# An order of work for a fused attention, soft MoE and routed MoE kernel: state loads on SyncE, the first step, pass changes and the first routed slots re-ordered

## The chip, the cores and the metric

The kernel runs on one core of one Trainium2 chip. The time is that of one launch on the device, in microseconds (us), from the runs' own clock; the profile's span is the time from the first to the last instruction of one profiled execution. The engines are TensorE (PE in the profile, its weight loads PEld), VectorE (DVE), ScalarE (ACT), GpSimd (POOL) and SyncE (SP), which only issues transfers here. Every engine works through its own instructions strictly in order.

## The reference

Three stages follow each other. N = 4 x (512 + 32) = 2176 tokens of 512 numbers, D = 64 per head, 8 heads, E = 8 experts with a hidden layer of F = 1024, all in float32.

```python
# stage 1: per batch and head, x (512 x 64) reads a state (32 x 64) and the state reads x
a  = softmax(x @ state.T / sqrt(64));  xread = a @ state
a2 = softmax(state @ x.T / sqrt(64));  sread = a2 @ x
x = concat([xread, sread], axis=2).transpose(0, 2, 1, 3).reshape(N, 512)
# stage 2: soft MoE, gates balanced by 8 Sinkhorn rounds
P = exp(x @ w_gate - max)
for _ in range(8):
    P /= P.sum(1); P /= P.sum(0); P *= N / E
x = sum(P[:, e:e+1] * (relu(x @ w1[e]) @ w2[e]) for e in range(E))
# stage 3: each token goes to its best expert alone
e = argmax(x @ w_gate2);  g = softmax(x @ w_gate2)[e] * sigmoid(x @ w_output_gate)[e]
out = g * (relu(x @ w1_2[e]) @ w2_2[e])
```

## The kernel before

**Tiling.** The 2176 tokens are 17 tiles of 128. Stage 2 goes over them in three passes, `PASSES` (first token, half width): (0, 384), (768, 384), (1536, 320), so passes have 6, 6 and 5 tiles. A pass has 32 steps: 8 experts by 4 quarters of 256 of the hidden layer. To keep float32 accuracy with the fast matmul type, every operand is split in a high part (a cast, on ScalarE) and a low part (operand minus high part, on VectorE or GpSimd), and each product is three matmuls (high by high, high by low, low by high; L481 to L483).

**A step** `s` has two halves. `mm1(s)` forms the hidden layer as seven products of a Strassen-like scheme, 6 matmuls each, from sums of quarters of the weights and of the tokens; between the products ScalarE copies and applies relu (L499, L490) and VectorE adds and forms low parts (L507 to L531, L494). In all steps but the first, the product numbered 2 comes fifth; in step 0 it comes second. `mm2(s)` multiplies the hidden layer by the second weights, tile by tile, 6 matmuls into one bank (L563 to L565), and VectorE adds the bank, weighted by the gate, into `acc` (L581; raw in the first experts, L572). The loop does `mm1` of step s and then `mm2` of step s - 1, so that TensorE has work while the hidden layer is finished.

**Operands one step ahead.** SyncE loads a quarter of the first weights (L418) and of the second (L421) into `rawb`. `prep_w1(s)` forms the sums on GpSimd (L434 to L437), the high parts on ScalarE (L438, L439, L442) and the low parts on GpSimd (L444, L446, L448); it runs inside step s - 1. `prep_w2(s)` casts on ScalarE (L458) and subtracts on GpSimd (L459); it runs inside `mm1(s)`, after its second product. Token operands of a pass are made by `xsums` and `xsplit`: seven operands, each cast on ScalarE (L406) and its low part formed on VectorE or GpSimd (L408); `pool` in `xsplit` names the operands whose low part is GpSimd's.

**Filling in.** `queue` is a list of closures; `pump` is called after every product and tile with the TensorE time that went by, and takes an item from the list whenever that credit reaches `pace`. The list holds the attention of batches 2 and 3 (`window(b)`, 17 items each: c0 to c4 of the two halves of the heads, and parts of the earlier batch), the 17 gate products, then the Sinkhorn rounds (`balance`), later the routing tables. In step 0 five items are taken directly in `between`. `todo` and the dictionary given to `step_mm2` do the same for the last two steps of a pass: the next pass's token operands (`xsplit`), and per finished tile `final_a` (store to x1d and x1p, L591 and L596, transposes L599, copy L601) and `final_b` (routing logits L610, L611).

**The order is written by hand** (`manual_schedule`): instructions are issued per engine in the order of the code, and what waits, waits for data or for a buffer. The first two batches' attention, with idle matmuls of no effect between, stands ahead of step 0. State of a batch comes by `load_state`: a memset on VectorE (L142), then four loads per half of the batch list, which ScalarE issues (L145). Batches 2 and 3 are loaded just ahead of step 0.

**Stage 3.** Tokens are routed to slots of 128 rows of one expert. VectorE builds tables (route parts `Rq[c][0..2]` for chunks c of tiles, L642 to L704; block tables in `blocks`, L1149 to L1187), TensorE turns them into row lists (`btab`: L715, then `indices`, L719 to L722), and GpSimd gathers a slot's rows (L834). `xT` transposes them (L842), with high part on ScalarE (L844) and low part on VectorE (L845); `m1` is the first layer (L855 to L857), `hT` transposes its relu (L869, L872, L873), `m2s` is the second layer (L880 to L882), scaled by the gate (L886) and scattered (L887). `load_w`/`split_w` bring the next expert's weights (L756, L806, L807). The gates of the slots come by a second table (`gmul` on GpSimd, L1198; `gtab` on TensorE, L715 into `pgat`). The head of this stage, slots 0 and 1, reads:

```python
m1(0, (seq(A[16], Rq[3][0]), seq(Bq[15], Bq[16]), seq(Rq[4][0], Rq[3][1])))
xT(1)
m1(1, (seq(Rq[4][1], blocks, lambda: load_w(2, 0)), lambda: hT(0)))
m2s(0, (None, btab, lambda: gather(2), seq(Rq[3][2], Rq[4][2], gmul)))
hT(1)
```

where the functions in brackets are called after the first, second, ... group of products of the layer.

Of the kernel before, what the change touches and what calls it, by code (L numbers as in the profile page):

```python
# [21 lines left out]
def tile_state_attention_moe_moe2(  # L22
# [117 lines left out]
    def load_state(b):  # L140
        stp = ap2.tile([P, G, P], F32, tag="stp", name=f"stp{b}")
        nc.vector.memset(stp, 0.0)  # L142
        sv = state[b].rearrange("(g q) s d -> q s g d", q=4)
        for q in range(4):
            nc.scalar.dma_start(out=stp[NS * q : NS * (q + 1), :, D * (q % 2) : D * (q % 2) + D], in_=sv[q])  # L145
        stps[b] = stp
# [250 lines left out]
    def xsplit(p, t, order=(0, 4, 3, 5, 1, 2, 6)):  # L397
        pool = (3, 1, 6) if p > 0 else ()
# [439 lines left out]
    def xT(sl):  # L838
# [5 lines left out]
        nc.scalar.copy(M["xh"], pv)  # L844
        nc.vector.tensor_tensor(out=M["xl"], in0=pv, in1=M["xh"].bitcast(F32), op=ALU.subtract)  # L845

    def m1(sl, hooks=()):
        ps2 = [bank(f"pm{sl}_{n}") for n in range(2)]
        hi, lo = M["xh"], M["xl"]
# [57 lines left out]
    with tc.manual_schedule():  # L907
# [9 lines left out]
        load_raw(0, 0)  # L917
        load_x(1, 0, accf[:, 2048:3072])
        load_state(1)
        gate_constants()  # L920
        load_raw(0, 1)
# [5 lines left out]
        load_x(1, 1)  # L927
        A1[0]()
# [21 lines left out]
        C0[3]()  # L950
        sums, T0 = xsums(0, accf)
        parts = xsplit(0, T0, (0, 1, 4, 3, 5, 2, 6))
        parts[0]()
        C1[3]()
        C0[4]()
        C1[4]()
        parts[1]()
        sums[0]()
        sums[1]()
        parts[2]()  # L960

        early = {0: [parts[3], sums[2]], 4: [parts[4]], 1: [parts[5], sums[3]], 2: [parts[6]]}
# [41 lines left out]
        def close_reads():  # L1004
# [6 lines left out]
            pace[0] = 5.6  # L1011
# [11 lines left out]
        def first_rows():  # L1023
# [3 lines left out]
            M["xh"], M["xl"] = (XR[:, 16384 + 512 * i : 16896 + 512 * i].rearrange("p (k t) -> p k t", k=KD) for i in (0, 1))  # L1027
# [8 lines left out]
        def step_mm1(s):  # L1036
            h = PASSES[s // NU][1]
            nxt = prep_w1(s + 1) if s < LAST else [lambda: None] * 2

            def between(i):  # L1040
                if s == 0:
                    for f in early.get(i, ()):
                        f()
                    if i in (0, 4, 1, 2, 3):
                        queue.pop(0)()
                if i == 1:
# [33 lines left out]
        queue += [gate([t]) for t in (6, 7, 0, 1, 2)] + spread(window(2), [3, 4, 5], 4)  # L1080
# [6 lines left out]
        pace[0] = 132.0 / (len(queue) - 5)  # L1087
# [3 lines left out]
        for s in range(3 * NU):  # L1091
# [29 lines left out]
            if p < 2:  # L1121
# [6 lines left out]
                step_mm2(s, {ts[2]: [a[0]], ts[3]: [a[1]], ts[4]: [b[0], a[2]], ts[5]: [b[1], a[3]]})  # L1128
# [4 lines left out]
            else:  # L1133
# [4 lines left out]
                step_mm2(s, {13: [A[12]], 14: [A[13], Bq[12]], 15: [A[14], Bq[13]],  # L1138
                             16: [piece[6], Bq[14], A[15], piece[7], lambda: xT(0)]})
# [70 lines left out]
        xT(1)  # L1210
        m1(1, (seq(Rq[4][1], blocks, lambda: load_w(2, 0)), lambda: hT(0)))
        m2s(0, (None, btab, lambda: gather(2), seq(Rq[3][2], Rq[4][2], gmul)))
# [61 lines left out]
```

## Time and profile before

| what | value |
|---|---|
| runs (3), us | 1844.94, 1847.14, 1849.73 |
| median | 1847.14 |
| the profiled execution: its own time / its span | 1845.63 / 1843.4 |
| TensorE busy, share of the span | 1787.8 us, 97% |
| VectorE / ScalarE / GpSimd busy | 1219.0 (66%) / 653.2 (35%) / 1086.4 us (59%) |
| mean granted clock of TensorE | 0.982 |

The span is the profiled execution from its first to its last instruction; its own time is 2.2 us longer, for what lies around the program. Busy time of TensorE counts an instruction at either clock as busy, so a stretch at half the clock looks full: the granted clock (1.00 is 2.4 GHz, 0.50 is 1.2 GHz) has to be read beside it. In timeline rows the bracket at the end gives the idle time of the engine just before the instruction and what ended it.

### The profile page before, as it was taken

How to read it: one execution, taken by the hardware profiler on the slowest of the kernel's cores; microseconds unless marked ns; L12 is line 12 of the kernel's file. 1: busy time of each engine (PE TensorE's matmuls, PEld its weight loads, DVE VectorE, ACT ScalarE, POOL GpSimd, SP SyncE). 2: the span in 40 equal slices, each digit the busy share in tenths (PEclk: the TensorE clock that was granted, in tenths of full speed). 3: DMA queues.
4: the chain of work that ended last, by engine and by line, in shares of the span. 5: the costliest groups of instructions: out<-in, count | busy, mean ns of one | idle time of the engine just before them, and what ended most of it. 6: DMA issues, size and time to landing. Idle time of an engine off the chain costs nothing.

```text
span 1843.4 us, 25573 instructions
## 1 busy us (share of the span) xinstructions
PE 1787.8 (97%) x9365; PEld 1594.5 (86%) x9365; DVE 1219.0 (66%) x2064; ACT 653.2 (35%) x1114; POOL 1086.4 (59%) x851
## 2 busy tenths in 40 slices
PE   7899998999999999999999999999999999899998
PEld 5889887899999889999999998889999998678886
DVE  5667679976676686666666666897666666545332
ACT  3334332233333433333333333333333334245333
POOL 1445445576776666666667765677787877222212
PEclk8799999999999999999999999999999999899999
DMA  4323421123222322112222222232222222335122
GB/s 108 82 92 81 114 65 55 60 69 101 60 71 68 121 74 68 66 66 65 69 98 69 69 69 92 81 126 81 81 81 81 81 80 81 115 106 195 44 83 91
DMA packets 126619, 154.67 MB, mean 84 GB/s; under 512 B 41424, under 2 KB 91600, under 8 KB 123920
## 3 DMA queue, kind: packets, MB, share of 16 engines
q1 hardware_dynamic: 121920, 142.41, 24.4%
q0 software_dynamic: 3280, 10.23, 1.6%
q8 instruction: 77, 1.26, 0.3%
q14 instruction: 62, 0.51, 0.1%
q10 hardware_dynamic: 1280, 0.26, 0.1%
HBM read 138.99 MB, written 14.42 MB: 83 GB/s over the span
## 4 chain that ended last, share of the span: by engine, by line
PE 71%; issue 12%; DVE 8%; DMA 4%; POOL 3%; ACT 1%; SPq 0%; POOLq 0%; DVEq 0%; ACTq 0%
PE py L563 12%; PE py L564 12%; PE py L565 12%; PE p L481 10%; PE p L483 10%; PE p L482 10%; DMA out_dram<-xst,si 2%; DVE HB L494 1%; DMA out_dram<-y,si 1%; DVE acc L581 1%; POOL XR L448 1%; PE psr L288 1%; PE pss L213 1%; POOL wl L459 1%; PE psg L310 1%
## 5 line engine op out<-in xcount | busy, mean ns | idle before, releaser
L459 POOL TENSOR_TENSOR wl<-rawb,wh 128x1024 fp32r<-128x1024 f32 x96 | 232.0, 2416 | 435.9 <-ACT wh L458 435.8
L481 PE MATMUL p<-XR 128*128 128x384 f32 (+1 forms) x1344 | 448.3, 334 | 9.0 <-ACT u L499 8.7
L483 PE MATMUL p<-XR 128*128 128x384 f32 (+1 forms) x1344 | 444.1, 330 | 9.2 <-POOL XR L448 8.1
L482 PE MATMUL p<-XR 128*128 128x384 f32 (+1 forms) x1344 | 442.7, 329 | 0.0
L563 PE MATMUL py<-wh,HB 128*128 128x512 f32 x1088 | 427.8, 393 | 2.2 <-DVE u L507 2.2
L565 PE MATMUL py<-wh,HB 128*128 128x512 f32 x1088 | 425.2, 391 | 0.0
L564 PE MATMUL py<-wl,HB 128*128 128x512 f32 x1088 | 425.1, 391 | 0.0
L581 DVE SCALAR_TENSOR_TENSOR acc<-py,PG,acc 128x512 f32<-128x512 f32 x461 | 321.2, 740 | 63.3 <-PE py L565 62.6
L448 POOL TENSOR_TENSOR XR<-sst,XR 128x1024 fp32r<-128x1024 f32 x96 | 252.4, 2629 | 56.4 <-ACT XR L442 56.4
L481 PEld LDWEIGHTS p<-XR 128*128 128x128 f32 x1344 | 256.1, 191 | 16.1 <-ACT u L499 8.8
L483 PEld LDWEIGHTS p<-XR 128*128 128x128 f32 x1344 | 255.6, 190 | 11.7 <-POOL XR L448 10.1
L494 DVE SCALAR_TENSOR_TENSOR HB<-u,HB 128x384 fp32r<-128x384 f32 (+1 forms) x192 | 186.7, 974 | 111.5 <-ACT HB L490 111.2
L482 PEld LDWEIGHTS p<-XR 128*128 128x128 f32 x1344 | 256.1, 191 | 3.3
L563 PEld LDWEIGHTS py<-wh,HB 128*128 128x128 f32 x1088 | 204.4, 188 | 44.5 <-DVE u L507 3.0
L565 PEld LDWEIGHTS py<-wh,HB 128*128 128x128 f32 x1088 | 204.2, 188 | 43.4
L564 PEld LDWEIGHTS py<-wl,HB 128*128 128x128 f32 x1088 | 204.4, 188 | 39.0
L499 ACT COPY u<-p 128x384 f32<-128x384 f32 (+1 forms) x96 | 44.3, 461 | 490.3 <-PE p L483 485.1
L444 POOL TENSOR_TENSOR XR<-rawb,XR 128x512 fp32r<-128x512 f32 x96 | 138.9, 1447 | 7.7 <-ACT XR L438 7.7
L442 ACT CAST XR<-sst 128x1024 fp32r<-128x1024 f32 x96 | 100.6, 1048 | 82.6 <-POOL sst L437 82.6
L490 ACT ACTIVATE HB<-u 128x384 fp32r<-128x384 f32 (+1 forms) x192 | 96.9, 505 | 77.9 <-DVE u L526 68.8
L507 DVE TENSOR_TENSOR u<-p,u 128x384 f32<-128x384 f32 (+1 forms) x96 | 51.2, 533 | 97.3 <-PE p L483 96.0
L490 ACT ACTIVATE HB<-p 128x384 fp32r<-128x384 f32 (+1 forms) x96 | 45.5, 474 | 181.6 <-PE p L483 181.6
(296 smaller groups left out, 2491.7 us busy)
## 6 DMA issues: line engine op xcount, KB each, us to landing
rawb<-in_moe_w_dram SPq DMA_DIRECT2D x192, 512.0 KB, 3.5
raw<-in_moe_w_dram SPq DMA_DIRECT2D x15, 1024.0 KB, 6.8
xb<-in_x_dram SPq DMA_DIRECT2D x60, 128.0 KB, 3.4
rawb<-in_moe_w_dram SPq DMA_DIRECT2D x5, 1024.0 KB, 5.0
x1d<-acc SPq DMA_DIRECT2D x16, 256.0 KB, 2.7
xtd<-xtm SPq DMA_DIRECT2D x4, 512.0 KB, 2.8
x1p<-acc SPq DMA_DIRECT2D x8, 256.0 KB, 3.1
xst<-xtd SPq DMA_DIRECT2D x1, 1536.0 KB, 9.5
```

What stands on the lines that cost most here:

```text
L444: nc.gpsimd.tensor_tensor(out=wop(s, 1, 0, 2).rearrange(r, k=KD), in0=raw[:, :, 0:P], in1=wop(s, 0, 0, 2).rearrange(r, k=KD).bitcast(F32), ...
L448: nc.gpsimd.tensor_tensor(out=wop(s, 1, 3, 4), in0=sst.rearrange("p a c -> p (a c)"), in1=wop(s, 0, 3, 4).bitcast(F32), op=ALU.subtract)
L459: nc.gpsimd.tensor_tensor(out=lo, in0=raw, in1=hi.bitcast(F32), op=ALU.subtract)
L481: nc.tensor.matmul(ps, wh, xh, start=start and k == 0, stop=False, skip_group_check=True)
L482: nc.tensor.matmul(ps, wh, xl, start=False, stop=False, skip_group_check=True)
L483: nc.tensor.matmul(ps, wl, xh, start=False, stop=stop and k == 1, skip_group_check=True)
L490: nc.scalar.activation(out=hh[:, f, half * h : (half + 1) * h], in_=c, func=AF.Relu)
L494: nc.vector.scalar_tensor_tensor(out=hl[:, f, q], in0=c, scalar=0.0, in1=hh[:, f, q].bitcast(F32), op0=ALU.max, op1=ALU.subtract)
L563: nc.tensor.matmul(ps, hh[:, j, r], whi[:, j, :], start=(j == 0), stop=False)
L564: nc.tensor.matmul(ps, hh[:, j, r], wlo[:, j, :], start=False, stop=False)
L565: nc.tensor.matmul(ps, hl[:, j, r], whi[:, j, :], start=False, stop=(j == 1))
L581: nc.vector.scalar_tensor_tensor(out=a, in0=ps, scalar=PG[:, t, e : e + 1], in1=a, op0=ALU.mult, op1=ALU.add)
```

## The change

It changes the order of work and which engine does some of it; what is computed stays the same.

- States of batches 2 and 3 are loaded from SyncE instead of ScalarE.
- In the prologue the first weights' loads and the gate constants come later, the second batch's loads earlier. Of the token operands of pass 0, the second is split ahead of the last attention parts; two of seven low parts go to GpSimd; the operands and sums are spread anew over step 0's products (`early`).
- The queue starts with gates 0 to 7, all of which are taken in step 0 (8 items instead of 5), and then the whole window of batch 2 without gates in it. The pace is 132/(length - 8), where it was 132/(length - 5): 132/56 and 132/59. Behind the attention it is 5.2 instead of 5.6.
- At pass changes (steps 32 and 64), `prep_w2` of the pass's first step and `prep_w1` of its second are called after tiles of the last `mm2` of the pass before, and no longer in the `mm1` of the first step.
- There are two buffers for a slot's transposed rows (`M["x"]`). `xT(0)` stands behind tile 14 and `xT(1)` behind tile 16 of the last `mm2`; before, `xT(0)` stood behind tile 16 and `xT(1)` behind `m1(0)`. In `m1(1)`, `hT(0)` comes ahead of `blocks`, and in `m2s(0)` the row table comes after the seventh group of products, the gather of slot 2, the rest of the routing and `gmul` after the eighth; they were behind the second, third and fourth.

```diff
@@ load_state
-            nc.scalar.dma_start(out=stp[...], in_=sv[q])
+            (nc.scalar if b < 2 else nc.sync).dma_start(out=stp[...], in_=sv[q])
@@ xsplit
-        pool = (3, 1, 6) if p > 0 else ()
+        pool = (3, 1, 6) if p > 0 else (3, 2)
@@ xT, m1
-        nc.scalar.copy(M["xh"], pv)
-        nc.vector.tensor_tensor(out=M["xl"], in0=pv, in1=M["xh"].bitcast(F32), op=ALU.subtract)
+        xh, xl = M["x"][sl == 1]
+        nc.scalar.copy(xh, pv)
+        nc.vector.tensor_tensor(out=xl, in0=pv, in1=xh.bitcast(F32), op=ALU.subtract)
...
-        hi, lo = M["xh"], M["xl"]
+        hi, lo = M["x"][sl == 1]
@@ prologue
         load_x(0, 1)
-        load_raw(0, 0)
         load_x(1, 0, accf[:, 2048:3072])
         load_state(1)
-        gate_constants()
-        load_raw(0, 1)
+        load_raw(0, 0)
...
         load_x(1, 1)
+        gate_constants()
+        load_raw(0, 1)
...
         C1[2]()
-        C0[3]()
         sums, T0 = xsums(0, accf)
         parts = xsplit(0, T0, (0, 1, 4, 3, 5, 2, 6))
         parts[0]()
+        C0[3]()
+        parts[1]()
         C1[3]()
         C0[4]()
+        sums[0]()
         C1[4]()
-        parts[1]()
-        sums[0]()
         sums[1]()
-        parts[2]()
-        early = {0: [parts[3], sums[2]], 4: [parts[4]], 1: [parts[5], sums[3]], 2: [parts[6]]}
+        early = {0: [parts[2], parts[3]], 4: [sums[2]], 1: [parts[4], sums[3]], 2: [parts[5], parts[6]]}
@@ close_reads
-            pace[0] = 5.6
+            pace[0] = 5.2
@@ first_rows
-            M["xh"], M["xl"] = (XR[:, 16384 + 512 * i : ...] for i in (0, 1))
+            M["x"] = [[h[:, o + 512 * i : ...] for i in (0, 1)] for h, o in ((XR, 16384), (HB, 2048))]
@@ step_mm1
-            nxt = prep_w1(s + 1) if s < LAST else [lambda: None] * 2
+            ahead = s > 0 and s % NU == 0
+            nxt = prep_w1(s + 1) if s < LAST and not ahead else [lambda: None] * 2
...
-                    if i in (0, 4, 1, 2, 3):
+                    for _ in range((1, 1, 1, 1, 3, 1, 0)[i]):
                         queue.pop(0)()
-                if i == 1:
+                if i == 1 and not ahead:
                     prep_w2(s)
@@ the queue
-        queue += [gate([t]) for t in (6, 7, 0, 1, 2)] + spread(window(2), [3, 4, 5], 4)
+        queue += [gate([t]) for t in (0, 1, 2, 3, 4, 5, 6, 7)] + window(2)
...
-        pace[0] = 132.0 / (len(queue) - 5)
+        pace[0] = 132.0 / (len(queue) - 8)
@@ the last step of a pass
-                step_mm2(s, {ts[2]: [a[0]], ts[3]: [a[1]], ts[4]: [b[0], a[2]], ts[5]: [b[1], a[3]]})
+                w1a, w1b = prep_w1(s + 2)
+                step_mm2(s, {ts[0]: [lambda: prep_w2(s + 1)], ts[1]: [w1a], ts[2]: [a[0]], ts[3]: [a[1], w1b],
+                             ts[4]: [b[0], a[2]], ts[5]: [b[1], a[3]]})
...
-                step_mm2(s, {13: [A[12]], 14: [A[13], Bq[12]], 15: [A[14], Bq[13]],
-                             16: [piece[6], Bq[14], A[15], piece[7], lambda: xT(0)]})
+                step_mm2(s, {13: [A[12]], 14: [A[13], Bq[12], lambda: xT(0)], 15: [A[14], Bq[13], piece[6]],
+                             16: [lambda: xT(1), Bq[14], A[15], piece[7]]})
@@ slots 0 and 1
-        xT(1)
-        m1(1, (seq(Rq[4][1], blocks, lambda: load_w(2, 0)), lambda: hT(0)))
-        m2s(0, (None, btab, lambda: gather(2), seq(Rq[3][2], Rq[4][2], gmul)))
+        m1(1, (Rq[4][1], lambda: hT(0), seq(blocks, lambda: load_w(2, 0))))
+        m2s(0, (None,) * 6 + (btab, seq(lambda: gather(2), Rq[3][2], Rq[4][2], gmul)))
```

Line numbers of the changed kernel lie one higher from `xT` on (L842 is L842, L845 is L846, L873 is L874), and some more at the end.

**First step, ScalarE.** The rows run from the end of the last attention part (copies into `xst`, L254) to the second weights' cast (`wh`, L458). Before:

```order
L254 COPY xst<-pso_402 128x256
L254 COPY xst<-pso_406 128x256
L406 CAST XR<-xst 128x768
L406 CAST XR<-acc 128x768
L145 DMA stp_427<-in_state_dram 32x2x64 x4
L145 DMA stp_433<-in_state_dram 32x2x64 x4
L499 COPY u_103<-p_0_446 128x384
L406 CAST XR<-acc 128x768
L490 ACTIVATE HB<-p_0_446 128x384
L406 CAST XR<-acc 128x768
L406 CAST XR<-xst 128x768
L458 CAST wh_496<-rawb 128x1024
```

and in the changed kernel:

```order
L254 COPY xst<-pso_405 128x256
L254 COPY xst<-pso_409 128x256
L499 COPY u_103<-p_0_444 128x384
L406 CAST XR<-acc 128x768 x2
L490 ACTIVATE HB<-p_0_444 128x384
L406 CAST XR<-acc 128x768
L458 CAST wh_506<-rawb 128x1024
L406 CAST XR<-xst 128x768
```

The eight state loads (two rows of four) are gone from the place ahead of the copy of `u`, one token operand is cast ahead of the attention's end, and between the copy of `u` and the weights' cast there are three token operands in both orders.

**First pass change, GpSimd.** The rows run from the last low part of the sums (L448) of the old pass's prepared step to the end of the preparation for the new pass's second step (`raw` and `xst` hold the new pass's tokens and sums). Before:

```order
L448 TENSOR_TENSOR XR<-sst,XR 128x1024
L408 TENSOR_TENSOR XR<-raw_2243,XR 128x768
L408 TENSOR_TENSOR XR<-xst,XR 128x768
L408 TENSOR_TENSOR XR<-raw_2243,XR 128x768
L459 TENSOR_TENSOR wl_5380<-rawb,wh_5379 128x1024
L434 TENSOR_TENSOR sst<-rawb 128x256
L435 TENSOR_TENSOR sst<-sst,rawb 128x256
L436 TENSOR_TENSOR sst<-rawb 128x256
L437 TENSOR_TENSOR sst<-rawb,sst 128x256
L444 TENSOR_TENSOR XR<-rawb,XR 128x512
L446 TENSOR_TENSOR XR<-rawb,XR 128x256
L448 TENSOR_TENSOR XR<-sst,XR 128x1024
```

and in the changed kernel:

```order
L448 TENSOR_TENSOR XR<-sst,XR 128x1024
L408 TENSOR_TENSOR XR<-raw_2243,XR 128x768
L459 TENSOR_TENSOR wl_5240<-rawb,wh_5239 128x1024
L434 TENSOR_TENSOR sst<-rawb 128x256
L435 TENSOR_TENSOR sst<-sst,rawb 128x256
L436 TENSOR_TENSOR sst<-rawb 128x256
L437 TENSOR_TENSOR sst<-rawb,sst 128x256
L408 TENSOR_TENSOR XR<-xst,XR 128x768
L444 TENSOR_TENSOR XR<-rawb,XR 128x512
L446 TENSOR_TENSOR XR<-rawb,XR 128x256
L448 TENSOR_TENSOR XR<-sst,XR 128x1024
L408 TENSOR_TENSOR XR<-raw_2243,XR 128x768
```

The weights' low part and the sums stand behind one token operand instead of three, the other two lie among and behind the weights' low parts.

**Tail, VectorE.** The rows show where the low half of the first slot's hidden layer (HB, L873 before, L874 in the change) stands relative to the block tables. Before, behind all of them (here their last four):

```order
L1184 TENSOR_SCALAR sm_13845<-sm_13844,sm_9838 128x24
L1185 TENSOR_SCALAR sm_13847<-sm_13845 128x24
L1186 TENSOR_TENSOR esel<-sm_13845,sm_13847 128x24
L1187 TENSOR_SCALAR flag<-sm_13829 128x1
L873 TENSOR_TENSOR HB<-pt_0_13888,HB 128x512
L821 UNCONDITIONAL_BRANCH
L873 TENSOR_TENSOR HB<-pt_1_13895,HB 128x512
```

and in the changed kernel ahead of them (L1154 is the first of the block tables there):

```order
L687 TENSOR_SCALAR rt_rb<-rt_rki 128x2
L688 CAST bk<-rt_rb 128x2
L874 TENSOR_TENSOR HB<-pt_0_13819,HB 128x512
L874 TENSOR_TENSOR HB<-pt_1_13826,HB 128x512
L1154 TENSOR_TENSOR sm_13843<-prank_13790,k_70 128x136
L1156 TENSOR_REDUCE sm_13839<-sm_13843 128x8
L1157 TENSOR_TENSOR sm_13839<-sm_13839,sm_10255 128x8
L1158 TENSOR_TENSOR sm_13844<-lowr,sm_13839 128x64
```

## Rows read from the trace of the kernel before

**Rows 1.** The page's 40 equal slices of the span: granted TensorE clock in tenths.

```profile
PEclk8799999999999999999999999999999999899999
```

**Rows 2.** Stretches: us, busy of PE, PEld, DVE, ACT, POOL; clock, DMA share, GB/s.

```profile
50.00:70.00 20.00, 19.34 (x72) 19.34 (x73) 11.91 (x20) 7.74 (x12) 9.46 (x8) 0.51 0.20 56
150.00:200.00 50.00, 50.00 (x293) 44.01 (x292) 36.46 (x64) 16.17 (x32) 20.00 (x16) 1.00 0.31 83
320.00:325.00 5.00, 3.78 (x12) 3.78 (x13) 4.83 (x11) 0.00 (x0) 4.61 (x6) 0.50 0.30 105
640.00:650.00 10.00, 7.86 (x35) 7.11 (x34) 7.69 (x14) 5.08 (x11) 7.10 (x5) 0.83 0.25 85
1150.00:1160.00 10.00, 6.79 (x34) 6.53 (x35) 7.08 (x14) 3.99 (x10) 7.70 (x6) 0.83 0.16 53
1580.00:1590.00 10.00, 8.66 (x44) 7.00 (x45) 4.48 (x20) 1.78 (x7) 0.00 (x0) 0.83 0.05 11
1600.00:1620.00 20.00, 16.33 (x79) 14.02 (x78) 12.37 (x49) 6.10 (x6) 5.81 (x6) 0.83 0.56 204
```

**Rows 3.** Timeline of the first step: start us, us, engine, instruction, [idle before <- releaser].

```profile
46.38 3.71 ACTq L145 DMA_DIRECT2D stp<-in_state_dram  x8
...
50.13 0.48 ACT L499 COPY u<-p 128x384 f32<-128x384 f32 x1 [5.05 <-DMA stp<-in_state_dram]
...
50.66 0.69 PE L481 MATMUL p<-XR 128*128 128x384 f32 x1 [8.73 <-ACT u L499]
...
54.23 0.96 DVE L408 TENSOR_TENSOR XR<-acc,XR 128x768 fp32r<-128x768 f32 x1 [0.95 <-ACT XR L406]
...
55.95 2.35 POOL L459 TENSOR_TENSOR wl<-rawb,wh 128x1024 fp32r<-128x1024 f32 x1 [21.61 <-ACT wh L458]
...
57.09 2.03 DVE L408 TENSOR_TENSOR XR<-xst,XR 128x768 fp32r<-128x768 f32 x1
...
69.62 2.37 POOL L448 TENSOR_TENSOR XR<-sst,XR 128x1024 fp32r<-128x1024 f32 x1 [4.51 <-ACT XR L442]
...
72.05 0.45 PE L483 MATMUL p<-XR 128*128 128x384 f32 x1 [1.15 <-POOL XR L448]
...
84.70 0.95 PE L310 MATMUL psg<-wg,xst 128*128 128x8 f32 x8
```

**Rows 4.** Timeline of the two pass changes.

```profile
628.88 1.82 POOL L408 TENSOR_TENSOR XR<-raw,XR 128x768 fp32r<-128x768 f32 x1 [7.76 <-DMA x1d<-acc]
...
635.38 2.38 POOL L459 TENSOR_TENSOR wl<-rawb,wh 128x1024 fp32r<-128x1024 f32 x1 [4.67 <-ACT wh L458]
...
645.61 0.45 PE L483 MATMUL p<-XR 128*128 128x384 f32 x1 [2.14 <-POOL XR L448]
...
1150.87 0.42 PE L483 MATMUL p<-XR 128*128 128x320 f32 x1 [1.16 <-POOL XR L444]
...
1154.36 0.41 PE L483 MATMUL p<-XR 128*128 128x320 f32 x1 [2.34 <-POOL XR L448]
```

**Rows 5.** Waits of TensorE, 250 to 360: us in total, times, longest us.

```profile
PE pscol L344 <- DVE sm L339: 9.6, 4, 5.2
```

**Rows 6.** Timeline of the first two slots of stage 3.

```profile
1580.69 0.50 PE L855 MATMUL pm<-XR 128*128 128x512 f32 x1 [1.68 <-ACT XR L844]
...
1582.07 0.79 PE L857 MATMUL pm<-XR 128*128 128x512 f32 x1 [0.64 <-DVE XR L845]
...
1593.01 0.50 PE L855 MATMUL pm<-XR 128*128 128x512 f32 x1 [1.32 <-ACT XR L844]
...
1604.22 0.50 PE L882 MATMUL pY<-XR,HB 128*128 128x512 f32 x1 [3.67 <-DVE HB L873]
...
1608.69 0.18 DVE L719 TENSOR_SCALAR gi<-ptab 128x24 int32<-128x24 f32 x1 [3.92 <-PE ptab L715]
...
1613.35 1.71 POOL L1198 TENSOR_TENSOR osg<-sm,gsplit 128x408 fp32r<-128x408 bf16 x2 [3.21 <-DVE gsplit L703]
...
1615.29 2.06 PE L715 MATMUL pgat<-osg,ohj 128*128 128x48 f32 x17
```

**Rows 7.** Waits of TensorE, 0 to 100.

```profile
PE psa L238 <- DVE e L233: 3.6, 3, 1.3
```

More of the change, by code (lines that the diff above doesn't have):

```diff
@@ L144, in load_state @@
         for q in range(4):
-            nc.scalar.dma_start(out=stp[NS * q : NS * (q + 1), :, D * (q % 2) : D * (q % 2) + D], in_=sv[q])
+            (nc.scalar if b < 2 else nc.sync).dma_start(out=stp[NS * q : NS * (q + 1), :, D * (q % 2) : D * (q % 2) + D], in_=sv[q])
         stps[b] = stp
@@ L1026, in first_rows @@
             M["y"] = [xst[:, 2560:3072], None]
-            M["xh"], M["xl"] = (XR[:, 16384 + 512 * i : 16896 + 512 * i].rearrange("p (k t) -> p k t", k=KD) for i in (0, 1))
+            M["x"] = [[h[:, o + 512 * i : o + 512 * i + 512].rearrange("p (k t) -> p k t", k=KD) for i in (0, 1)]
+                      for h, o in ((XR, 16384), (HB, 2048))]
             M["hh"], M["hl"] = (HB[:, 1024 * i : 1024 * i + 1024].rearrange("p (j t) -> p j t", j=NJ) for i in (0, 1))
```

## The prediction

> **What bounds it now.** I read four views in this order. The page's slices show TensorE's granted clock at 9 nearly everywhere and at 7 or 8 only at the front and in the tail [rows 1]; TensorE itself is busy 97% of the span. So the time is TensorE's work, plus the places where it stops or runs at the low clock. A table of stretches then finds those places [rows 2]: the steady stretch 150 to 200 is 50.00 busy of 50.00 at clock 1.00, and there nothing can be won. The first step (50 to 70) is busy too, but at 0.51, that is at 1.2 instead of 2.4 GHz; it gives up 20 x 0.49 = 9.8 us. The pass changes (640, 1150) and two places of the tail (1580, 1600) show 0.83, and 320 to 325 shows 0.50 with only 3.78 of 5.00 busy. The timeline then names what each place waits for [rows 3, 4, 6], and the chain of waits gives the sums [rows 5, 7].
>
> In the first step the story starts on ScalarE [rows 3]: eight state loads sit in its queue from 46.38, for 3.71 us, because they wait for a memset behind VectorE's work. The copy of u, next in that queue, starts at 50.13 after 5.05 idle, and TensorE stands 8.73 us before 50.66, its product long done. Then it works on at the low clock. GpSimd's chain (second weights, sums, low parts) is late in turn, and step 1's second product gets its operand only at 72.05.
>
> At the pass changes [rows 4] GpSimd is idle 7.76 and 4.67 us before the end of a pass and then late: TensorE stops 2.14, and 1.16 + 2.34 at the second change. In the tail [rows 6] TensorE stops 1.68 and 0.64 at the first slot's rows, 1.32 at the second's, and 3.67 for the hidden layer's low half, which stands on VectorE behind the block tables.
>
> **The change, part by part.** The sum is made against the profiled execution, 1845.63 us (span 1843.4). The median of the runs, 1847.14, lies 1.5 above it.
>
> *Front (state loads, first step, gates).* With the loads on SyncE, the u copy follows its product: that ended at 50.66 - 8.73 = 41.93, so u starts near 42.1, 8.0 earlier than 50.13. From u to the second weights' low part on GpSimd the trace has 5.8 us (50.13 to 55.95); the new order has the same three operands in between, and part of the 5.8 waits for half-clock products, so I take 5.6: it starts at 47.7, 8.25 earlier. From there to the end of the low part that step 1 waits for, the trace has 69.62 + 2.37 - 55.95 = 16.0 us. In it are 4.51 of waiting for ScalarE's cast, which waits on TensorE's half-clock products; that goes. One more operand's low part comes onto GpSimd in this stretch, 1.82 us by its row at the pass change [rows 4]; the other moved one runs ahead of the weights, in idle time. So 16.0 - 4.5 + 1.8 = 13.3, end at 61.0 instead of 72.0: 10.9 won. GpSimd then bounds this step and TensorE stops in pieces, so three more gates (8 instead of 5) fall in idle time: 3 x 0.95 = 2.85 at most, nothing at least; I take 2.4, since an 11 us shorter step still has stops of some 5 us by this working. Those stops may hold the clock low for a while beyond what the chain hides: 0 to half of the 9.8, and I take 1.5, because the products behind GpSimd's chain are hidden by it. Front: 10.9 + 2.4 - 1.5 = 11.8, ends 5 (rival A below, with one gate's 0.8 less hidden) and 13.8 (all gates, no clock loss).
>
> What stands behind the moved loads on SyncE is the next w2 quarter (L421), which needs a buffer that the weights' low part frees later anyway: nothing. The prologue's other moves (weights' first load behind the x and state loads) are covered by the idle matmuls there; GpSimd was idle 21.61 before its low part at 55.95, so a load some us later costs nothing.
>
> What a DMA on ScalarE costs is shown by the row: the issue takes 3.71 us, but the copy behind it is held 5.05 and TensorE 8.73 [rows 3]. The Trainium skill, "DMA: Bandwidth & Descriptors", section "Issuing engines are not separate DMA queues", says that issuing from several engines saves only the sequencer's time, usually small. By it the move would be worth 3.71, the front 3.7 + 2.4 - 1.5 = 4.6, and the time about 1826. I keep the row: it shows a queue that waits, not only issues.
>
> *Sinkhorn (265 to 325).* Before, TensorE waits 9.6 us in 4 for VectorE's chain [rows 5], the longest 5.2, and 320 to 325 has clock 0.50 [rows 2]. The change moves gates out of the attention windows and sets the pace behind it at 5.2 instead of 5.6, so the column sums come at other points of the steps. VectorE is 4.83 of 5.00 busy there, so the chain itself gets no shorter. The bounds: all of the longest wait and most of the clock go (7), or one more wait of 2 comes. I take 2.5, about the half-clock loss of that one stretch (5 x 0.50).
>
> *Pass changes.* GpSimd's work for the new pass's first two steps (low part 2.38, sums, low parts) moves ahead into its 7.76 + 4.67 of idle time. What can go: at the first change 2.14 and 10 x 0.17 = 1.7 of clock, at the second 1.16 + 2.34 + 1.7: together 9.0. Less 1 for VectorE and ScalarE, whose copies and accumulations for the last tiles now stand behind four more casts: 8. Ends 4 (half of the waits only move) and 9.
>
> *Tail.* Gone: 1.68 + 0.64 + 1.32 + 3.67 = 7.3 of stops [rows 6], as both slots' rows are ready before the pass ends and the hidden layer stands before the block tables; and the low clock, 10 x 0.17 + 20 x 0.17 = 5.1 [rows 2]. New: the gate products now start late. From the indices at 1608.69 to the end of the gate products 1613.35 + 1.71 = 1615.06 there are 6.37 us that ran beside the first slot's second layer; now only its last three matmuls and one transpose block lie beside them (about 1.7), so TensorE stops some 4.7 before the gate table at 1615.29, and the clock costs about 2 after it. 12.4 - 4.7 - 2 = 5.7, ends 2 (the stop 8, nothing hidden) and 9 (fully hidden second table, one clock loss left). The block tables keep cover: behind the hidden layer come the second slot's last 12 products and the first 21 of the second layer, 33 of the 44 that take 8.66 us at 1580 to 1590, so 6.5 us for some 30 small VectorE operations of about 0.2 us [rows 2, 6].
>
> Sum: 11.8 + 2.5 + 8 + 5.7 = 28.0. 1845.63 - 28.0 = 1817.6, and 1.5 to the median: **1819**.
>
> **The rivals.** (A) *GpSimd and VectorE hold each other up.* VectorE's low part took 2.03 at 57.09 beside GpSimd's work and 0.96 at 54.23 without [rows 3]. With two more such parts on GpSimd in the stretch that it bounds, up to half of VectorE's 11.91 busy us there [rows 2], 6 us (my guess for the share with two inputs in SBUF), would be added to the chain: front 5.8, sum 22, about 1825. For it: that row. Against: VectorE loses the same two parts. The Trainium skill, "SBUF — State Buffer", section "SBUF: two separate sides", calls the shared port pair an exclusive lock under which the other engine blocks; by that rule the 2.03 is a block, and the row agrees.
>
> (B) *The pass-change split gives nothing*, since it only trades places: ScalarE's casts for the new weights then stand behind the last tiles' copies, and the wait for GpSimd turns into one for ScalarE. 28 - 8 = 20: about 1827. For it: TensorE's stops there are short, and any delay of 2 us on ScalarE restores them. Against: 12.4 us of GpSimd idle time.
>
> (C) *More:* the long Sinkhorn wait goes whole (7), the front and tail reach 13.8 and 7: with 8, a sum of 36, about 1811.
>
> (D) *Slower: attention without gates in between starves.* Window items of batch 2 stand in the stream without gates. When an item waits for VectorE or ScalarE, TensorE stops as in the front, 3.6 us in 3, 1.2 each [rows 7]. If each of the 34 items of both windows waited so, that is 41: 41 - 28 = 13 slower, about 1860. It decides when the spacing of dependent items falls below the latency of the softmax between them. Three items at the new pace are 3 x 132/56 = 7.1 us apart; before 3 or 4 items with a pace of 132/59, 6.7 to 8.9. Against it: at 6.7 the trace shows no stop (50.00 of 50.00) [rows 2].
>
> **How the numbers follow.** The forecast has 0.60, A 0.17, B 0.10, C 0.07, D 0.04, and 0.02 is left for A and B at once with the Sinkhorn part and the tail at their lower ends: 28 - 6 - 8 - 4.5 - 3.7 = 6, near 1841. The four terms' ends taken together as independent give about -10 and +6 around 28, so 1813 to 1829; to take in C and A with a further miss I set 1811 to 1832. About 0.3% (5.5 us, 1841.6) is what a measurement of this kernel can tell from no change. Of A and B some 0.04 lies above that bound together with another miss. Faster 0.94 - 0.04 = 0.90, same 0.06, slower 0.04.
>
> **What would show it.** Right: no state load in ScalarE's queue near 46; the stop of 8.73 gone; the low part that step 1 waits for done near 61; clock 1.00 and no wait on GpSimd at 640 and 1150; no wait for the slots' rows or the hidden layer in the tail, and instead one of 4 to 6 us before the gate table, released by GpSimd. Wrong: a new wait on VectorE in the windows of batches 2 and 3 (D), GpSimd rows in the first step much longer than 1.8 and 2.4 (A), a wait on ScalarE's casts in the new pass (B), or a Sinkhorn sum of waits well over 10.

## The result, and the profile after

The changed kernel takes 1824.32 us (median of 4 runs, 1822.61 to 1827.49) against 1846.74 before (now of four runs): a ratio of 0.9879, with a 95% interval of 0.9859 to 0.9899. It is 22.4 us faster. Forecast were 1819 and a range of 1811 to 1832; the gain that was forecast, 28, is a quarter too large. The profiled execution is the slowest of the four runs, 1827.49 with a span of 1825.4, so its gain is 18.0 us; a second profile of the same kernel (below) gains 22.3.

The page's clock slices, which answer to [rows 1], have lost the 8 in the tail; the two low digits at the front stand:

```profile
PEclk8799999999999999999999999999999999999999
```

Stretches at the places of [rows 2], moved by what was won ahead of them (us, busy of PE, PEld, DVE, ACT, POOL; clock, DMA share, GB/s):

```profile
40.00:50.00 10.00, 10.00 (x60) 10.00 (x59) 9.28 (x16) 5.14 (x8) 3.27 (x2) 0.74 0.66 164
50.00:70.00 20.00, 20.00 (x87) 19.93 (x87) 11.18 (x19) 7.24 (x14) 15.93 (x13) 0.62 0.23 63
...
250.00:300.00 50.00, 45.23 (x219) 39.98 (x217) 44.39 (x96) 13.46 (x24) 24.83 (x22) 0.93 0.17 51
...
630.00:640.00 10.00, 10.00 (x59) 10.00 (x59) 8.30 (x20) 5.38 (x12) 2.50 (x2) 1.00 0.02 6
1136.00:1146.00 10.00, 10.00 (x67) 9.74 (x66) 8.13 (x23) 5.33 (x13) 3.36 (x2) 1.00 0.00 0
...
1580.00:1590.00 10.00, 8.66 (x51) 7.34 (x50) 7.90 (x42) 2.94 (x4) 1.00 (x1) 1.00 0.22 65
1590.00:1600.00 10.00, 6.54 (x24) 5.96 (x25) 5.19 (x16) 3.80 (x2) 4.80 (x5) 0.56 0.93 336
```

TensorE no longer stops in the first step (10.00 of 10.00, 20.00 of 20.00), but it still works there at a clock of 0.62. Both pass changes are full at 1.00. The tail has one bad stretch left, at 0.56. TensorE's waits over the whole span (us in total, times, longest) name what is left:

```profile
PE pscol L344 <- DVE sm L339: 7.3, 5, 2.5
PE pgat L715 <- POOL osg L1203: 4.8, 1, 4.8
PE py L563 <- DVE u L507: 4.5, 3, 1.9
PE psa L238 <- DVE e L233: 3.6, 3, 1.2
PE prank L672 <- DVE cum L667: 2.6, 1, 2.6
PE p L483 <- POOL XR L448: 2.1, 3, 1.2
PE psx L202 <- DMA xb<-in_x_dram: 1.9, 2, 1.1
PE py L563 <- DVE acc L579: 1.9, 1, 1.9
```

Gone are the 8.7 for the copy of u and most of the waits on GpSimd's low part (8.1 in all before). New are 4.8 before the gate table, 1.9 for VectorE's accumulation in the second pass (behind the first change), and 2.6 instead of 1.0 for the rank counts.

**Where the 18 us come from.** Each step has one copy of u (L499), so the start of that row, step for step in both profiles, tells how far the changed kernel is ahead: 262.46 against 252.31 at step 10 is 10.15. Away from the places (steps 17 to 31, 36 to 64, 72 to 95) the lead stays constant to 0.01 us. All kernels below are read this way. The last column of numbers is the tail, from step 69 on, up to the difference of the spans.

| kernel | lead at step 10 | Sinkhorn, 10 to 17 | first change, 17 to 36 | second, 36 to 69 | tail | span ahead |
|---|---|---|---|---|---|---|
| forecast | 11.8 | +2.5 | together | +8 | +5.7 | 28 |
| changed, first profile | 10.15 | -1.66 | +2.39 | +2.70 | +4.4 | 18.0 |
| changed, second profile | 13.87 | -1.58 | +2.36 | +3.08 | +4.6 | 22.3 |
| state loads on ScalarE | 4.51 | -1.30 | +0.79 | +3.98 | +4.4 | 12.4 |
| pass changes as before | 13.89 | -1.66 | -0.06 | -0.02 | +3.7 | 15.8 |
| tail as before | 13.94 | -4.64 | +2.38 | +2.69 | +0.1 | 14.5 |
| no gates in step 0 | 3.88 | -2.84 | +2.40 | +2.84 | +4.6 | 10.9 |
| gates of step 0 spread | 10.29 | -3.21 | +2.36 | +3.98 | +4.4 | 17.8 |
| gate values early | 11.78 | -1.53 | +2.41 | +3.98 | +6.1 | 22.7 |
| low parts on VectorE | 13.73 | -1.56 | +2.41 | +2.66 | +4.5 | 21.7 |
| pace 5.6 | 9.55 | -0.04 | +2.41 | +3.97 | +4.6 | 20.5 |
| pace 6.0 | 17.00 | +2.59 | +2.36 | +3.10 | +4.7 | 29.7 |
| before, state loads on SyncE | 5.71 | -1.18 | -0.01 | -0.02 | +0.2 | 4.7 |
| pace 6.0 and gate values early | 15.23 | +0.99 | +2.35 | +4.00 | +5.9 | 28.5 |

The second change comes out between 2.7 and 4.0 from profile to profile, and one first change at 0.79. The difference is the granted clock of one stretch: with the loads on ScalarE the 80 matmuls of step 34 take TensorE 17.41 us at a clock of 0.91, in the first profile 15.80 at 1.00; and where the second change brings 4.0, TensorE is busy for about 13.35 us in step 65 at 1.00, where the first profile has 14.18 at 0.94.

### The profile page after: what moved, and what is told of

Same layout as the page of the kernel before. It is cut to its first block, busy times and chain, and to the rows that moved or that the text cites. A ratio compares the mean times of both kernels' runs of the same rounds, so it can differ in the third digit from the quotient of the medians.

```text
span 1825.4 us, 25577 instructions
## 1 busy us (share of the span) xinstructions
PE 1784.9 (98%) x9365; PEld 1593.4 (87%) x9365; DVE 1218.4 (67%) x2062; ACT 653.9 (36%) x1114; POOL 1091.9 (60%) x853
## 4 chain that ended last, share of the span: by engine, by line
PE 76%; issue 10%; DVE 8%; DMA 4%; POOL 1%; ACT 0%; SPq 0%; POOLq 0%; DVEq 0%; ACTq 0%
PE py L563 12%; PE py L564 12%; PE py L565 12%; PE p L481 11%; PE p L483 11%; PE p L482 11%; DMA out_dram<-xst,si 2%; DMA out_dram<-y,si 1%; DVE HB L494 1%; PE psg L310 1%; PE pss L213 1%; DVE acc L581 1%; PE psr L288 1%; DVE sm L347 1%; PE pl L610 0%
## 5 line engine op out<-in xcount | busy, mean ns | idle before, releaser
L459 POOL TENSOR_TENSOR wl<-rawb,wh 128x1024 fp32r<-128x1024 f32 x96 | 232.1, 2418 | 432.8 <-ACT wh L458 432.8
L483 PE MATMUL p<-XR 128*128 128x384 f32 (+1 forms) x1344 | 442.0, 329 | 2.1 <-POOL XR L448 2.1
L448 POOL TENSOR_TENSOR XR<-sst,XR 128x1024 fp32r<-128x1024 f32 x96 | 252.4, 2630 | 47.4 <-ACT XR L442 45.4
L483 PEld LDWEIGHTS p<-XR 128*128 128x128 f32 x1344 | 254.8, 190 | 3.0 <-POOL XR L448 3.0
L494 DVE SCALAR_TENSOR_TENSOR HB<-u,HB 128x384 fp32r<-128x384 f32 (+1 forms) x192 | 174.4, 911 | 111.6 <-ACT HB L490 111.3
L499 ACT COPY u<-p 128x384 f32<-128x384 f32 (+1 forms) x96 | 44.4, 462 | 475.3 <-PE p L483 475.2
```

The lines of the kernel that those rows point to most:

```text
L448: nc.gpsimd.tensor_tensor(out=wop(s, 1, 3, 4), in0=sst.rearrange("p a c -> p (a c)"), in1=wop(s, 0, 3, 4).bitcast(F32), op=ALU.subtract)
L459: nc.gpsimd.tensor_tensor(out=lo, in0=raw, in1=hi.bitcast(F32), op=ALU.subtract)
L483: nc.tensor.matmul(ps, wl, xh, start=False, stop=stop and k == 1, skip_group_check=True)
L494: nc.vector.scalar_tensor_tensor(out=hl[:, f, q], in0=c, scalar=0.0, in1=hh[:, f, q].bitcast(F32), op0=ALU.max, op1=ALU.subtract)
```

## The experiments

**The changed kernel again.** No edit.

> The changed kernel again, unedited, with a second profile. Theory A (the four places of the first profile): it is earlier than the kernel before by about 10.1 us ahead of the Sinkhorn rounds, then loses 1.7 in them, wins 2.4 and 2.7 at the two pass changes and 4.5 in the tail, about 1824 in all. Rival B: the parts in the Sinkhorn rounds and the first step differ from execution to execution (the four runs lay 5 us apart), and a second profile shows another split, with the pass changes and the tail alone repeating.

Measured: 1826.06 (ratio 0.9885, 0.9868 to 0.9902), lead 22.3 in its profile. The pass changes and the tail repeat, and here the Sinkhorn part does too; the front does not, 13.87 against 10.15. The reason stands ahead of step 0. Stretches of the first profile and then of the second:

```profile
12.00:16.00 4.00, 4.00 (x22) 3.88 (x21) 1.35 (x3) 0.00 (x0) 0.22 (x1) 0.50 1.02 248
16.00:20.00 4.00, 4.00 (x20) 4.00 (x21) 1.44 (x4) 1.10 (x2) 2.60 (x4) 0.50 0.77 157
```

```profile
12.00:16.00 4.00, 3.84 (x36) 3.61 (x36) 2.64 (x4) 1.10 (x2) 1.26 (x2) 1.00 1.17 267
16.00:20.00 4.00, 3.16 (x28) 2.87 (x28) 2.95 (x6) 2.90 (x6) 2.74 (x4) 1.00 0.60 145
```

Behind the first waits for x, the clock fell to 0.50 at 12 in one execution and stayed at 1.00 in the other, with the same program: 36 matmuls were done in four us instead of 22, and the second exponential of the attention starts at 16.16 instead of 20.03. That is the 3.7 us between the two leads. Of the profiles of the table, the first of the changed kernel, those with no gates, spread gates, early gate values and pace 5.6, and both kernels with the prologue of before have the low-clock prologue (second exponential at 18.8 to 20.4), the others the full-clock one (15.8 to 16.2). Leads at step 10 are therefore compared within one kind: 9.6 to 11.8 is the front of the change where both kernels have the low-clock prologue and gates in step 0.

**State loads back on ScalarE.**

```diff
-            (nc.scalar if b < 2 else nc.sync).dma_start(out=stp[...], in_=sv[q])
+            nc.scalar.dma_start(out=stp[...], in_=sv[q])
```

> The changed kernel with the loads of the states of batches 2 and 3 issued from ScalarE again. Theory A: the copy of u waits for the memset (now at 42.25 on VectorE) and the 3.7 us of issue, so TensorE stops about 5 us near 42 to 46; some 5 us slower than the changed kernel, 1829. Rival B: the stop of before came from VectorE's order alone, which the other edits have already changed; then it is under 2 us slower, 1826. Rival C: the stop also keeps the clock low longer, as before, and the whole 10 us of the front go, 1834.

Measured: 1833.24 (0.9919, 0.9898 to 0.9939), 9.4 us less lead at step 10 than the second profile (both with the full-clock prologue). Its timeline:

```profile
39.17 4.21 ACTq L145 DMA_DIRECT2D stp<-in_state_dram  x8
43.42 0.48 ACT L499 COPY u<-p 128x384 f32<-128x384 f32 x1 [6.27 <-DMA stp<-in_state_dram]
...
43.96 0.69 PE L481 MATMUL p<-XR 128*128 128x384 f32 x1 [5.45 <-ACT u L499]
```

The stop is 5.45, as theory A had it, but the price is 9.4, rival C's: all of 44 to 68 runs at 0.50 in this profile, while the second profile of the changed kernel is at 0.94 from 60 to 68. So the stop is paid twice here, once as idle time and once as low clock behind it. Issuing alone takes 4.21.

**One part alone.** The kernel before, with the states of batches 2 and 3 loaded from SyncE (the same line, the other way).

> The kernel before with one part of the change: states of batches 2 and 3 loaded from SyncE. Theory A: the stop of 8.7 us goes and with it part of the low clock; most of the front comes from this line alone, 7 to 10 us ahead at step 10, 1838 to 1841. Rival B: without the other reordering the first step then waits for GpSimd's chain or for the operands' low parts on VectorE, and it is 4 us or less ahead.

Measured: 1841.79 (0.9963, 0.9949 to 0.9977): 5.7 ahead at step 10, between the two theories; a stop of 3.6 for the copy of u stays, since that copy still stands behind a token operand's cast there. The line is worth 9.4 with the new order behind it and 5.7 with the old one.

**Pass changes as before** (`ahead = False`, and no preparation in the last `mm2`).

> The changed kernel with the pass-change preparation back in the new pass's first step. Theory A: the two gains of 2.4 and 2.7 us go, 1829, and TensorE waits for GpSimd's low part (L448) again at both changes, 2 to 4 us each time with a clock under 1.0 behind it; the new waits of the changed kernel there (1.9 for VectorE's accumulation, 2.6 for the rank counts) go too. Rival B: these new waits come from elsewhere and stay; then it is 8 to 9 us slower, 1833.

Measured: 1829.98 (0.9914, 0.9891 to 0.9938). Both gains are gone, to 0.06 us, and the lead is flat from step 17 to 95. TensorE's waits around the second change, 1100 to 1200:

```profile
PE p L483 <- POOL XR L448: 4.0, 3, 2.4
PE p L483 <- POOL XR L444: 1.2, 1, 1.2
PE prank L672 <- DVE cum L667: 1.0, 1, 1.0
```

GpSimd's low parts are waited for again, the rank counts 1.0 instead of 2.6, and the 1.9 for the accumulation (behind the first change) is gone: the new waits belong to the split ahead, theory A.

**Tail as before** (the order of tiles and functions of the kernel before, both buffers kept).

> The changed kernel with the order of the tail of before (both buffers for the transposed rows kept). Theory A: 4.5 us slower, 1829, with waits for the slots' rows and for the hidden layer's low half (about 3.7 and 3.7) in place of the 4.8 for the gate products, and a clock of 0.8 to 0.9 there. Rival B: the second buffer alone gives part of it, and it is 2 us or less slower.

Measured: 1829.79 (0.9902, 0.9876 to 0.9928); the tail's gain falls from 4.6 to 0.1, so the second buffer alone gives nothing. Its waits, 1540 to 1640:

```profile
PE pY L883 <- DVE HB L874: 3.6, 1, 3.6
PE pm L856 <- ACT XR L845: 2.4, 2, 1.7
PE pm L856 <- ACTq L826: 1.4, 1, 1.4
PE pm L856 <- ACT HB L845: 1.3, 1, 1.3
```

**Gates out of step 0.**

```diff
-                    for _ in range((1, 1, 1, 1, 3, 1, 0)[i]):
-                        queue.pop(0)()
...
-        pace[0] = 132.0 / (len(queue) - 8)
+        pace[0] = 132.0 / len(queue)
```

> The changed kernel with no gate products in step 0 (all 8 go later, pace 132/64). Theory A: the clock falls in step 0 because three gates stand in a row there (24 matmuls of 8 columns, the fall comes some 2 us after the first); without gates it stays near 1.00 from 40 to 60, TensorE is then bound by GpSimd's chain and stops near 50 to 57 for it, and the gates cost 8 x 0.81 = 6.5 us later: some 3 us slower than the changed kernel, 1828. Rival B: the clock falls there with or without gates (it also fell before, with TensorE standing); then 0.5 from 41 on, step 0 shorter by the gates, no stop for GpSimd or a short one, and 0 to 3 faster.

Measured: 1832.05 (0.9911, 0.988 to 0.9942). First two stretches of the second profile of the changed kernel, then of this one:

```profile
36.00:44.00 8.00, 8.00 (x50) 8.00 (x49) 7.05 (x13) 4.02 (x8) 1.85 (x1) 0.78 0.64 164
44.00:52.00 8.00, 8.00 (x33) 8.00 (x32) 7.13 (x6) 2.95 (x5) 7.22 (x5) 0.50 0.48 119
```

```profile
36.00:44.00 8.00, 5.58 (x26) 3.30 (x25) 7.04 (x14) 5.64 (x11) 0.00 (x0) 1.00 0.25 79
44.00:52.00 8.00, 4.24 (x18) 3.01 (x18) 7.56 (x8) 4.68 (x8) 5.05 (x3) 1.00 0.60 135
```

```profile
54.40 0.69 PE L482 MATMUL p<-XR 128*128 128x384 f32 x1 [4.25 <-POOL XR L408]
...
62.16 0.58 PE L483 MATMUL p<-XR 128*128 128x384 f32 x1 [1.99 <-POOL XR L448]
```

(The first profile, whose prologue is like this one's, has 0.74 over 40 to 50.) Theory A's mechanism: without the gates the clock holds at 1.00 up to 52, and TensorE stops for GpSimd instead, 4.25 us for a token operand's low part and 1.99 for the last low part of the weights' sums; behind the first stop its clock is low too (0.57 over 52 to 60). So with the gates it is the low clock that hides GpSimd, and without them GpSimd ends the step. The price was expected at 3 and is 6.3 by the lead at step 10 (10.15 to 3.88, both with the low-clock prologue), near what the 8 gates cost elsewhere: 8 x 0.81 = 6.5.

**Gates of step 0 spread** (1, 1, 1, 2, 1, 1, 1 behind the products).

> The changed kernel with the 8 gates of step 0 spread as 1, 1, 1, 2, 1, 1, 1 behind its seven products (it has three in a row behind the second). Theory A: no three in a row, so the clock stays near 1.00 in step 0, GpSimd's chain then ends it, about 3 us earlier than now: 1822. Rival B: the clock falls all the same, no difference: 1825 within 1.5.

Measured: 1826.36 (0.9879, 0.9862 to 0.9895), the front as in the first profile (10.29). The clock falls later, near 48, just behind the one place with two gates in a row, and step 1's copy of u is only 0.6 earlier than in the first profile (a lead of 7.14 instead of 6.52), of which 0.14 is left at step 10: rival B's time, though the fall moved as theory A had it.

**The two low parts back on VectorE** (`pool = (3, 1, 6) if p > 0 else ()`).

> The changed kernel with the two low parts of pass 0's operands on VectorE again. Theory A: TensorE's own work at 1.2 GHz ends the first step, not GpSimd's chain, so GpSimd finishing some 2 to 4 us earlier brings nothing; VectorE is later by two parts, 0 to 3 us slower. Rival B: the chain on GpSimd ends the step, as predicted; then 2 us faster.

Measured: 1824.2 (0.9873, 0.9857 to 0.989), 13.73 at step 10 against 13.87: no difference. That alone doesn't decide between the theories, for the edit hardly moved the end of GpSimd's chain: the last low part ends at 59.53 instead of 59.90 in the second profile, since it waits for ScalarE's cast (2.93 us instead of 1.74). The second profile decides it: the matmul that needs this low part starts at 61.19, 1.3 behind its end, and in neither profile of the changed kernel does TensorE wait for GpSimd in the first step. So TensorE's own work ends it.

**Pace 5.6, and pace 6.0** (`pace[0]` in `close_reads`).

> The changed kernel with the pace behind the attention at 5.6, as before, instead of 5.2. Theory A: the loss of 1.6 us between steps 10 and 17 (13.9 won before it, 12.3 after it) comes from where the pace puts the column sums; at 5.6 it is gone, 0 to 1, and the kernel is 1.5 faster than the changed one. Rival B: VectorE is full there at any pace (98 of 110 us busy in both kernels), and what the front wins is partly given back whatever the pace: the loss stays at 1 to 3.

> The changed kernel with the pace behind the attention at 6.0. Theory A: the column sums' positions matter; the sum of the waits for them moves by 2 us or more from the 6.9 to 7.3 of the changed kernel, up or down, and the loss between steps 10 and 17 with it. Rival B: within 1 us of what the kernel at 5.6 shows.

Measured: 1821.57 (0.9851, 0.9834 to 0.9867) at 5.6, and 1821.75 (0.9861, 0.9844 to 0.9877) at 6.0. Waits for the column sums at 5.6, and then at 6.0:

```profile
PE pscol L344 <- DVE sm L339: 9.6, 4, 5.2
```

```profile
PE pscol L344 <- DVE sm L339: 6.7, 3, 3.2
```

At 5.6 the waits are those of the kernel before [rows 5], and the loss of the Sinkhorn part is gone (-0.04); at 6.0 the part wins 2.59. So the new pace goes with the loss, theory A. The sum of these waits doesn't rank them, though: 5.2 has 7.3 and loses 1.66. TensorE's busy time over the same 566 matmuls, steps 10 to 17, does. The kernel before, the first profile, and then step 10 alone in the first and the second profile:

```profile
262.46:386.88 124.42, 114.52 (x566) 102.05 (x565) 113.21 (x202) 36.48 (x65) 75.13 (x70) 0.97 0.18 60
252.31:378.39 126.08, 116.59 (x566) 102.30 (x565) 115.83 (x199) 36.51 (x65) 75.54 (x70) 0.97 0.19 59
...
252.31:272.04 19.73, 18.08 (x86) 15.82 (x85) 17.42 (x40) 5.56 (x10) 9.97 (x8) 0.91 0.16 54
...
248.59:266.71 18.12, 16.48 (x86) 14.68 (x85) 15.88 (x36) 5.56 (x10) 9.97 (x8) 1.00 0.20 59
```

TensorE is idle for 9.5 us instead of 9.9, but busy for 2.1 more: the same matmuls ran at a lower clock. The mean clock doesn't show it (0.97 in both), because before much of the low clock lay on TensorE's own wait, where it costs nothing (step 13: 0.85, with 18.03 of 23.19 busy). One stretch at the low clock costs 1.4 to 1.6, as in step 10, and how many there are differs between executions of one program. At 5.2 the nine profiles have 9.2 to 9.5 idle and 116.3 to 119.6 busy, with the clock under 1.00 in two or three of steps 10 to 12; at 5.6 three profiles have 9.9 idle and 114.5 to 115.7 busy (the kernel before with the loads on SyncE, at 5.6 too, loses 1.18, with step 10 at 0.91); at 6.0 two have 7.7 idle and 114.2 to 115.8. So the pace sets the waits, and at 5.2 the low clock behind them falls on more of the work in every profile; what it adds from one execution to the next stays open.

**Gate values early.**

```diff
-        m1(0, (..., seq(Rq[4][0], Rq[3][1])))
-        m1(1, (Rq[4][1], lambda: hT(0), seq(blocks, lambda: load_w(2, 0))))
-        m2s(0, (None,) * 6 + (btab, seq(lambda: gather(2), Rq[3][2], Rq[4][2], gmul)))
+        m1(0, (..., seq(Rq[4][0], Rq[3][1], Rq[3][2])))
+        m1(1, (Rq[4][1], lambda: hT(0), seq(blocks, lambda: load_w(2, 0)), seq(Rq[4][2], gmul)))
+        m2s(0, (None,) * 6 + (btab, lambda: gather(2)))
```

> The changed kernel with the last two chunks' gate values ahead of the row table on VectorE (one behind the ranks of chunk 3, one behind the block tables) and the gate products on GpSimd right behind them. Theory A: the wait of 4.8 before the gate table is VectorE's order and falls to about 2, the clock of 0.56 behind it rises: 3 to 6 us faster than the changed kernel, 1819 to 1822. Rival B: VectorE is full there, so the hidden layer's low half or the row table comes later by as much, and the time stays within 1.5.

Measured: 1823.11 (0.9865, 0.9844 to 0.9887), tail +6.1 instead of +4.6. Its wait, and its stretch where the changed kernel has 0.56:

```profile
PE pgat L715 <- POOL osg L1203: 0.8, 1, 0.8
```

```profile
1590.00:1600.00 10.00, 7.56 (x32) 5.56 (x32) 6.17 (x6) 6.08 (x4) 3.33 (x4) 0.93 1.00 362
```

The wait falls by 4.0, but only 1.5 arrive: a new wait of 1.3 for the rank counts (3.9 in 2 instead of 2.6 in 1) and one of 1.1 for the slots' rows show VectorE late elsewhere. The wait went as theory A had it, the time as rival B.

**Both together** (5 runs).

> The changed kernel with the pace of 6.0 and the last gate values ahead of the row table. Theory A: the two gains add by their places: against the second profile of the changed kernel 4.2 us between steps 10 and 17 (2.6 won instead of 1.6 lost) and 1.5 in the tail, so some 5.7 below the changed kernel's 1824 to 1826: 1819. Rival B: one of them was an effect of its own execution's clock; then 1821 to 1824, as each alone.

Measured: 1817.43 (0.9844, 0.983 to 0.9857), 31.0 us below the 1848.43 of the kernel before beside it and the fastest version here. In its profile, which has the full-clock prologue, the Sinkhorn part is +0.99, not the +2.59 of pace 6.0 alone (step 11 is at 0.92 here and at 1.00 there), and the tail +5.9. That is theory A's time but not quite its places: against the second profile 2.6 come between steps 10 and 17 instead of 4.2, 1.3 in the tail, and 1.4 at the front and 0.9 at the second change, which theory A did not count.

## Why the prediction was right, and where it was off

**Front (11.8; measured 10.15, with a prologue like that of before).** The removal of the stop was right: no state load in ScalarE's queue, the copy of u at 40.79, no stop. The first step of the changed kernel's first profile:

```profile
40.79 0.48 ACT L499 COPY u<-p 128x384 f32<-128x384 f32 x1 [0.60 <-PE p L483]
...
42.53 2.95 PE L310 MATMUL psg<-wg,xst 128*128 128x8 f32 x24
...
43.98 1.85 POOL L408 TENSOR_TENSOR XR<-acc,XR 128x768 fp32r<-128x768 f32 x1 [10.01 <-ACT XR L406]
...
44.15 2.50 DVE L393 TENSOR_TENSOR acc<-xst 128x768 f32<-128x768 f32 x1
...
45.80 0.52 PE L482 MATMUL p<-XR 128*128 128x384 f32 x1
...
48.58 2.71 POOL L459 TENSOR_TENSOR wl<-rawb,wh 128x1024 fp32r<-128x1024 f32 x1 [2.75 <-ACT wh L458]
...
51.25 2.54 POOL L408 TENSOR_TENSOR XR<-xst,XR 128x768 fp32r<-128x768 f32 x1
...
60.65 2.36 POOL L448 TENSOR_TENSOR XR<-sst,XR 128x1024 fp32r<-128x1024 f32 x1 [1.36 <-ACT XR L442]
...
64.47 0.52 PE L483 MATMUL p<-XR 128*128 128x384 f32 x1
```

GpSimd's second weights start at 48.58 (predicted 47.7) and its last low part ends at 63.0 (predicted 61.0). The step that failed is the next one, "GpSimd then bounds this step and TensorE stops in pieces": TensorE is never idle there. It works at 1.2 GHz (0.62 over 50 to 70, where before it was 0.51), and that is what ends the step: the matmul that needs the last low part (L483, the third of step 1's second product) starts at 64.47, 1.5 behind that part's end, where before it started with it, at 72.05. That the two ends lie so close is luck, and so is that the 1.5 is the size of the clock term in the sum: there it stood for what stops leave behind, and there are no stops. Of the front's 10.15, 7.6 come from this matmul and the other 2.6 by step 10, near the 2.4 taken for the three extra gates. Gates are nearly free in this step, as predicted, though not because they fall in idle time: with all 8 left out, GpSimd holds the same matmul until 62.16, so they cost 2.3 there, and the front loses 6.3 without them.

**Sinkhorn (+2.5; measured -1.66 and -1.58).** The step that failed is "I take 2.5, about the half-clock loss of that one stretch". The wait of 5.2 did go, and with it the 0.50 at 320 to 325, as assumed; but five of up to 2.5, one of 1.9 for VectorE's u and a clock of 0.93 over 250 to 300 came in their place. I priced the waits that would vanish and not those that the new positions bring, nor the low clock behind them: the waits fell by 0.4 in all, and TensorE's work took 2.1 longer. The pace goes with it (-0.04 at 5.6). The bound of -2 held for the first two profiles but not for all of the kernels at 5.2 (-4.64, -3.21 and -2.84 in three of them).

**Pass changes (+8; measured +5.1 and +5.4).** The mechanism is right: the clock is 1.00 and nothing waits for GpSimd there. The term was too large because "less 1 for VectorE and ScalarE" was 3.5: TensorE, now earlier, meets VectorE's accumulation (1.9) and the rank counts (1.6 more). Just behind the second change the clock is under 1.00 in both profiles (0.94 and 0.92 in step 65); where it is 1.00 in other profiles, that change brings 4.0 instead of 2.7 and 3.1.

**Tail (+5.7; measured +4.4 and +4.6).** The new wait before the gate table was predicted as 4.7, released by GpSimd, and is 4.80. Off was only "the clock costs about 2 after it":

```profile
1593.46 3.83 PE L715 MATMUL pgat<-osg,ohj 128*128 128x48 f32 x17 [4.80 <-POOL osg L1203]
```

The gate table took 2.06 before [rows 6], so 1.8 more here, and the nine matmuls behind it start 0.43 apart instead of 0.23, another 1.8: 3.6 in all. (0.56 over the ten us of 1590 to 1600 would give 4.4, but TensorE stands for a part of them.) The four stops counted there went as said.

**The rivals.** D did not come: no wait in the windows of batches 2 and 3 (TensorE 50.00 of 50.00 in each 50 us from 100 to 250). B falls by the run without the split. C did not come either, as the Sinkhorn part lost. A is half true: beside each other, GpSimd's L408 took 2.54 (1.82 at [rows 4]) and its L459 2.71 (2.35 at [rows 3]), which is the 1.1 that its chain was longer than predicted, and VectorE's sum (L393) 2.50, where it took 0.95 before; but nothing followed in the time, as TensorE was later still. The Trainium skill, "SBUF — State Buffer", section "SBUF: two separate sides", would have each block the other for whole instructions; the row agrees in kind: L393 starts at 44.15 beside a GpSimd row of 43.98 to 45.83 and ends 0.82 behind it. The rule priced nothing here, as the 64.47 shows. The Trainium skill, "DMA: Bandwidth & Descriptors", section "Issuing engines are not separate DMA queues", would have the move save the issue alone. The run with the loads back on ScalarE differs: 4.21 to issue, 9.4 of time.

**The sum.** Place by place, with like prologues, each term came out smaller than taken: 10.15 - 1.66 + 5.1 + 4.4 = 18.0 instead of 28. The second profile's 22.3 has 3.7 from the clock of its prologue, of which the prediction had no term. How much of the 22.4 between the medians is of that kind no run shows; it may be luck that the medians lie nearer to the forecast than the first profile does.

## What to carry to other kernels

A transfer issued from a compute engine's queue costs what it holds up, not its issue (4.21 us here, against 9.4 and 5.7 of time in the two runs): look at what stands behind it there, and add the low clock that the stop leaves behind. When a stop is removed, price what the earlier engine meets next; here that was 3.5 us of new waits at the pass changes. Read such a change by the lead at a row that occurs once per step: it splits the sum by place, and shows at once which part differs from execution to execution. Within a place, set TensorE's idle time and its busy time over the same matmuls beside each other: the mean clock doesn't tell whether the low clock lay on work or on a wait.

## What was not expected of the hardware

TensorE's clock fell while TensorE was never idle: at 45, behind three gates in a row (24 matmuls of 8 columns, 2.95 us), from a pitch of 0.17 to 0.32 us, with TensorE 10.00 of 10.00 busy; with the gates left out it held 1.00 through 36 to 52, although TensorE was busy only 9.82 of these 16 us. And the same program has its clock at 0.50 in one execution and at 1.00 in another from 12 to 20, and is 3.7 us earlier for it; what decides, and whether the kernel before has the full-clock prologue at times too, stays open, since its one profile shows the low one. Later stretches differ in the same way: step 10 of the same program took 19.73 at 0.91 and 18.12 at 1.00, with the same 86 matmuls.
